# Fewer TensorE tiling changes in a joint image and text attention block: full-size text transposes, adjacent text mods, gate rows beside the text scores, text keys in four row tiles

## The chip, the cores and the metric

The kernel runs on one core of one Trainium2 chip. The time is device microseconds of that core for one execution, as the median of several executions. "Span" is the time of the profiled execution from its first to its last instruction, about 1.8 us shorter than the device time of the same execution.

The records give each TensorE matmul a tile form. In the profile of the kernel before they are 128x128 (687 of 1,051 matmuls), 128x32 (254), 128x64 (76), 64x128 (27), 32x128 (6) and, once, 18x128. In what follows 128x32 is called four column tiles, 64x128 two row tiles and 32x128 four row tiles, because the matmuls of one such form are seen to overlap: four on 128x32 tiles start 2 to 5 ns apart, mostly 3 or 4, and each lasts 286 ns by its modelled end. The change is about how often the form changes.

## The reference, cut to what matters

There are B = 2 batches of Ni = 256 image tokens and Nt = 32 text tokens, D = 1152, all bf16.

```
mod_i = silu(c) @ wmod_img ;  mod_t = silu(c) @ wmod_txt     # shift, scale, gate of each stream
hi = layernorm(x_img) * (1 + sci) + shi ;  ht = layernorm(x_txt) * (1 + sct) + sht
qkvi = hi @ wqkv_img ;  qkvt = ht @ wqkv_txt
scores = concat(qt, qi) @ concat(kt, ki)^T * D**-0.5 ;  p = softmax(scores) ;  a = p @ concat(vt, vi)
out_i = x_img + gai * (ai @ wo_img) ;  out_t = x_txt + gat * (at @ wo_txt)
```

Fourteen matrices of 1152x1152 (2.65 MB each) are read once. That is nearly all of the traffic.

## The kernel before

All weights are loaded by one in-order queue into five slots in on-chip memory, each of which is used several times. A load into a slot is not issued before the last reader of its old content is done; the loads behind it in the queue wait too. In the profile before, the scale rows end at 56.25 us and the load into their slot is issued at 56.29.

```python
    # ... cut: the loads of the image scale and value weights into slots 0 and 1 ...
    w_sh_i = load_w(2, wmod_img, 0)          # first argument: the slot
    w_q_i = load_w(3, wqkv_img, 0)
    w_sh_t = load_rows(0, wmod_txt, 0)
    w_k_i = load_w(4, wqkv_img, D)
    w_sc_t = load_w(1, wmod_txt, D)          # text scale weights
    w_q_t = load_w(2, wqkv_txt, 0)
    w_k_t = load_w(3, wqkv_txt, D)
    w_v_t = load_w(1, wqkv_txt, 2 * D)       # text value weights: the slot of the text scale weights
    w_ga_i = load_w(0, wmod_img, 2 * D)      # image gate weights
    w_ga_t = load_w(2, wmod_txt, 2 * D)
    w_o_i = load_rows(3, wo_img, 0)
    w_o_t = load_rows(1, wo_txt, 0)
```

TensorE's program order is fixed. The text work is hung into the nine blocks of the image query and key projections:

```python
    qk_img(w_q_i, 0, {1: (txt_ln,), ..., 6: (txt_transposes,), 8: (txt_shift_part(6, KT),)})
    qk_img(w_k_i, 1, {1: (txt_shift_split, txt_rows_scale,),
                      6: (txt_rows_shift, txt_cols_shift, txt_modulate),
                      8: (lambda: qk_txt(0, w_q_t),)})
    qk_txt(1, w_k_t)
    # ... cut: helpers ...
    scores_txt()
    scores_img(0)
    img_gate()
    scores_img(1)
    v_txt()
    p_transposes(0)
    txt_gate()
    # ... cut: attn_pair(G[0], G[1]); p_transposes(1); two more pairs; the output projections
```

`txt_rows_scale` multiplies the conditioning vector by the text scale weights: 36 matmuls on 128x32 tiles, 1.3 us. It is the last reader of that slot. `img_gate` does the same with the image gate weights. Transposes are matmuls too: the small ones use 64x128 or 32x128 tiles. In `attn_pair` the text keys are added with two row tiles of 64 rows.

## Time and profile before

| | before |
|---|---|
| time, median (range) | 120.37 us (120.02 to 120.63, 3 runs) |
| span of the profile | 118.6 us |
| TensorE busy | 95% of the span |
| weight stream | about 410 GB/s almost until the last weights |

From the page: the span in 40 slices (TensorE's busy tenths, its granted clock in tenths, the DMA engines' busy tenths, GB/s), then the chain of waits that ended last, by engine.

```profile
PE   4988899999999999999999999999999999999990
PEclk9999999999999999999999999999999999999998
DMA  4999999999999999999999999999999996220223
GB/s 104 382 392 399 404 410 406 413 412 411 411 389 384 413 412 410 405 413 411 412 413 412 410 407 413 412 404 412 405 408 411 412 389 219 109 89 16 99 50 100
...
PE 86%; DMA 8%; DVE 2%; SPq 1%; issue 1%; DVEq 0%
```

After the first slices TensorE never rests, and the chain is almost all TensorE. The stream has no hole either: two resources are full at once, and only one of them is on the chain.

The timeline of the load queue (start and duration of the issue in us, then what is loaded):

```profile
56.29 0.85 SPq L89 DMA_DIRECT2D t<-in_wqkv_txt_dram  x1
62.68 0.82 SPq L89 DMA_DIRECT2D t<-in_wmod_img_dram  x1
```

The text value weights are asked for at 56.29 us, as soon as the scale rows are done; the image gate weights at 62.68. The stream is still busy with the text key weights then.

The timeline of TensorE, some groups (start, us from the first start to the last end, operation, tile form, shape, count):

```profile
46.72 0.43 PE L64 MATMUL tpt<-ident,xn_t 64*128 64x64 bf16 x9
...
54.96 1.29 PE L61 MATMUL gps<-t,sT 128*32 128x288 bf16 x36
...
66.00 0.67 PE L61 MATMUL gps<-hl,pick 128*32 128x288 bf16 x16
...
77.26 3.21 PE L61 MATMUL sps<-qkT 128*32 128x288 bf16 x36
80.40 1.29 PE L61 MATMUL gps<-t,sT 128*32 128x288 bf16 x36
81.62 2.38 PE L61 MATMUL sps<-qkT 128*128 128x288 bf16 x18
...
89.17 0.54 PE L61 MATMUL aps<-pT,v_t 64*128 64x288 bf16 x6
```

In order: the small text transposes, the scale rows (54.96), the shift rows (66.00), the text scores with image scores(0), the image gate rows (80.40), image scores(1), and the text keys of the first pair. None of these lines has an idle time in brackets at its end: TensorE waits for nothing. (Some matmul records can be missing from a trace, so a count may be one or two short.)

The single matmul records of this profile say what a change of form costs here. Successive matmuls start 216 ns apart (512 columns) or 123 ns apart (288 columns). Where the form changes and nothing is waited for, the distance is about 310 ns (309 to 311, from 512 columns) or 219 ns (214 to 219, with 288), so 91 to 96 ns more, and the step after a return to 128x128 is 10 ns longer (226 or 133 ns). That is what was measured; what happens in the engine meanwhile is not shown.

### The profile page before, as it was taken

How to read it: one execution, taken by the hardware profiler on the slowest of the kernel's cores; microseconds unless marked ns; L12 is line 12 of the kernel's file. 1: busy time of each engine (PE TensorE's matmuls, PEld its weight loads, DVE VectorE, ACT ScalarE, POOL GpSimd, SP SyncE). 2: the span in 40 equal slices, each digit the busy share in tenths (PEclk: the TensorE clock that was granted, in tenths of full speed). 3: DMA queues.
4: the chain of work that ended last, by engine and by line, in shares of the span. 5: the costliest groups of instructions: out<-in, count | busy, mean ns of one | idle time of the engine just before them, and what ended most of it. 6: DMA issues, size and time to landing. Idle time of an engine off the chain costs nothing.

```text
span 118.6 us, 2515 instructions
## 1 busy us (share of the span) xinstructions
PE 112.1 (95%) x1051; PEld 64.0 (54%) x1059; DVE 75.3 (63%) x157; ACT 41.8 (35%) x86; POOL 10.3 (9%) x31
## 2 busy tenths in 40 slices
PE   4988899999999999999999999999999999999990
PEld 1335544445674444445444457877876666666660
DVE  2568592063966799999999540048685666666571
ACT  4799620041752524323039233345327620000000
POOL 7110000000000000000000000000409017000000
PEclk9999999999999999999999999999999999999998
DMA  4999999999999999999999999999999996220223
GB/s 104 382 392 399 404 410 406 413 412 411 411 389 384 413 412 410 405 413 411 412 413 412 410 407 413 412 404 412 405 408 411 412 389 219 109 89 16 99 50 100
DMA packets 18613, 40.86 MB, mean 345 GB/s; under 512 B 1019, under 2 KB 1547, under 8 KB 18603
## 3 DMA queue, kind: packets, MB, share of 16 engines
q1 hardware_dynamic: 17728, 39.56, 85.7%
q0 software_dynamic: 480, 0.89, 2.2%
q10 hardware_dynamic: 395, 0.26, 0.7%
q8 instruction: 8, 0.13, 0.4%
q14 instruction: 2, 0.02, 0.0%
HBM read 39.38 MB, written 1.34 MB: 343 GB/s over the span
## 4 chain that ended last, share of the span: by engine, by line
PE 86%; DMA 8%; DVE 2%; SPq 1%; issue 1%; DVEq 0%
PE ps L61 52%; PE vps L61 15%; DMA t<-in_wmod_img_dram 8%; PE gps L61 6%; PE aps L61 6%; PE sps L61 5%; PE sc_ps L61 1%; PE pT_ps L64 1%; SPq L104 1%; DVE tmp L629 1%; DVE o L630 0%; DVE scc L217 0%; SPq L108 0%; PE tpt L64 0%; PE tp L64 0%
## 5 line engine op out<-in xcount | busy, mean ns | idle before, releaser
L61 PE MATMUL ps<-xT_i,t 128*128 128x512 bf16 x157 | 35.6, 380 | 0.3
L61 PEld LDWEIGHTS <-t 128*128 128x128 bf16 x324 | 20.4, 98 | 19.2 <-issue 0.7
L395 DVE SCALAR_TENSOR_TENSOR acc_sh<-t,sTf,acc_sh 128x1152 f32<-128x1152 bf16 x16 | 21.3, 1404 | 0.0
L61 PE MATMUL ps<-t,aT 128*128 128x384 bf16 (+3 forms) x153 | 20.2, 308 | 0.0
L61 PE MATMUL vps<-t,hS_i 128*128 128x512 bf16 (+1 forms) x106 | 17.8, 325 | 0.3 <-DVE hS_i L248 0.2
L61 PEld LDWEIGHTS <-aT 128*128 128x128 bf16 (+1 forms) x153 | 13.0, 101 | 7.1 <-issue 0.5
L61 PEld LDWEIGHTS <-hS_i 128*128 128x128 bf16 x108 | 9.0, 98 | 8.8 <-DVE hS_i L248 0.3
L629 DVE TENSOR_TENSOR tmp<-ps,gb 128x384 bf16<-128x384 f32 (+2 forms) x13 | 6.8, 526 | 6.3 <-PE ps L61 6.3
L346 ACT ACTIVATE qkT<-ps 128x512 bf16<-128x512 f32 (+2 forms) x11 | 6.2, 561 | 12.1 <-PE ps L61 12.1
L61 PE MATMUL wps<-warm 128*128 128x512 bf16 x25 | 7.7, 458 | 1.6 <-DVE unit L132 1.5
L481 POOL DMA_DIRECT2D mod_scratch<-g_sb x4 | 2.5, 634 | 76.6 <-ACT g_sb L174 76.6
L348 ACT CAST qkT<-ps 128x512 bf16<-128x512 f32 (+2 forms) x11 | 5.9, 554 | 8.3 <-PE ps L61 8.3
L172 DVE CAST v_i<-vps 128x512 bf16<-128x512 f32 x5 | 3.5, 692 | 8.2 <-PE vps L61 8.2
L553 DVE TENSOR_TENSOR half<-sps,half 64x288 f32<-64x288 f32 x1 | 0.4, 448 | 9.0 <-ACT half L552 9.0
L587 DVE TENSOR_SCALAR aT<-aps,svc 128x288 bf16<-128x288 f32 x9 | 4.5, 518 | 2.6 <-PE aps L61 2.5
L61 PEld LDWEIGHTS <-sT 128*32 128x32 bf16 x180 | 4.5, 96 | 2.8 <-issue 2.2
L174 ACT CAST v_i<-vps 128x512 bf16<-128x512 f32 x4 | 2.3, 580 | 10.0 <-PE vps L61 10.0
L61 PE MATMUL sps<-qkT 128*128 128x288 bf16 (+1 forms) x54 | 5.6, 288 | 0.0
L61 PEld LDWEIGHTS <-warm 128*128 128x128 bf16 x26 | 2.6, 111 | 5.2 <-issue 2.1
L61 PE MATMUL aps<-pT,v_i 128*128 128x288 bf16 x36 | 5.3, 288 | 0.0
L589 ACT ACTIVATE aT<-aps,svc 128x288 bf16<-128x288 f32 x9 | 4.1, 498 | 3.0 <-PE aps L61 2.9
L61 PE MATMUL gps<-t,sT 128*32 128x288 bf16 x144 | 5.1, 287 | 0.0
(104 smaller groups left out, 108.0 us busy)
## 6 DMA issues: line engine op xcount, KB each, us to landing
t<-in_wqkv_txt_dram SPq DMA_DIRECT2D x3, 2592.0 KB, 16.5
t<-in_wmod_img_dram SPq DMA_DIRECT2D x2, 2592.0 KB, 13.9
t<-in_wqkv_img_dram SPq DMA_DIRECT2D x2, 2592.0 KB, 20.1
t<-in_wmod_txt_dram SPq DMA_DIRECT2D x2, 2592.0 KB, 15.5
t<-in_wmod_txt_dram SPq DMA_DIRECT2D x3, 864.0 KB, 14.7
t<-in_wo_img_dram SPq DMA_DIRECT2D x3, 864.0 KB, 12.3
t<-in_wo_txt_dram SPq DMA_DIRECT2D x3, 864.0 KB, 11.4
t<-in_wqkv_img_dram SPq DMA_DIRECT2D x3, 576.0 KB, 9.2
```

The lines of the kernel that those rows point to most:

```text
L61: return pin(nc.tensor.matmul(*a, **k))
L64: return pin(nc.tensor.transpose(*a, **k))
L104: nc.sync.dma_start(x_i[:, b * TPB:(b + 1) * TPB, :], x_img[b].rearrange("(p t) d -> p t d", t=TPB))
L172: nc.vector.tensor_copy(out_ap, in_ap)
L174: nc.scalar.copy(out_ap, in_ap)
L346: nc.scalar.mul(out_ap, in_ap, SCALE)
L348: nc.scalar.copy(out_ap, in_ap)
L395: pin(eng.scalar_tensor_tensor(acc[:, b, :], w[:, kt, :], sTf[:, kt, b:b + 1], acc[:, b, :], op0=ALU.mult, op1=ALU.add))
L481: nc.gpsimd.dma_start(gsc[si, b, :].rearrange("(g j) -> g j", g=NGG), g_sb[b:P:32, :])
L587: nc.vector.tensor_scalar(dst, tiles[(b, dt)][:], bias, None, op0=ALU.add)
L589: nc.scalar.activation(dst, tiles[(b, dt)][:], ACT.Identity, bias=bias)
L629: nc.vector.tensor_mul(tmp[:, 0:n], ps[:, 0:n], gb[:, b, c0:c0 + n])
```

## The change

The intent is to change the form less often.

- The text is normalised into two halves, one above the other, so that five full transposes replace nine small ones.
- The scale rows go beside the shift rows, both 128x32.
- Image scores(0) come before the text scores, so that text scores and gate rows, both 128x32, are adjacent.
- The probabilities of the text queries are transposed full size, from a zero-padded tile, and both batches one after the other.
- The text keys use four row tiles of 32 rows.

```diff
     def txt_transposes():
-        tpt = ps_tr.tile([P, KT, NTT], bf, tag="tr")
-        for kt in range(KT):
-            tr(tpt[:, kt, :], xn_t[:, kt * P:(kt + 1) * P], ident[0:NTT, 0:NTT])
+        tpt = ps_tr.tile([P, KH, 2, NTT], bf, tag="tr")
+        for k in range(KH):
+            tr(tpt[:, k].rearrange("p h t -> p (h t)"), xn_t[:, k * P:(k + 1) * P], ident[:])
 # ... cut: the two halves of xn_t, the padded tiles and their memsets ...
-    qk_img(w_k_i, 1, {1: (txt_shift_split, txt_rows_scale,),
-                      6: (txt_rows_shift, txt_cols_shift, txt_modulate),
+    qk_img(w_k_i, 1, {1: (txt_shift_split,),
+                      6: (txt_rows_scale, txt_rows_shift, txt_cols_shift, txt_modulate),
 # ... cut: p_transposes with full-size transposes of the text tile ...
-            first = key in t1
-            r0, (b, dt) = 64 * (n % 2), key
-            mm((t1 if first else t0)[key][:], lhsT=v_t[r0:r0 + 64, dt * P:(dt + 1) * P],
-               rhs=pTs[b][r0:r0 + 64, 2, :], start=first, stop=not first, tile_position=(r0, 0))
+            first, (b, dt) = key in t1, key
+            r0 = 64 * (n // 2 % 2) + NT * b
+            mm((t1 if first else t0)[key][:], lhsT=v_t[r0:r0 + NT, dt * P:(dt + 1) * P],
+               rhs=pTs[b][r0:r0 + NT, 2, :], start=first, stop=not first, tile_position=(r0, 0))
-    scores_txt()
     scores_img(0)
+    scores_txt()
     img_gate()
     scores_img(1)
     v_txt()
     p_transposes(0)
+    p_transposes(1)
     txt_gate()
 # ... cut: each attn_pair takes three tiles of each batch ...
```

More of the change, by code (lines that the diff above doesn't have):

```diff
@@ L150 @@
     nc.gpsimd.memset(shT32[:], 0.0)
+    PBW = 3 * P
+    pb_tiles = [act.tile([P, PBW], bf, name="pb%d" % i) for i in range(2 * B)]
+    pb_txt = act.tile([P, PBW], bf, name="pbt")
+    KH = (KT + 1) // 2
+    xn_t = act.tile([P, KH * P], bf)
+    nc.gpsimd.memset(pb_txt[:], 0.0)
+    nc.gpsimd.memset(xn_t[NTT:P, (KT - KH) * P:KH * P], 0.0)
+    for t in pb_tiles:
+        nc.gpsimd.memset(t[:, NI:PBW], 0.0)
+    ident2 = const.tile([P, P], bf)
+    nc.gpsimd.tensor_copy(ident2[:, 0:P - NT], ident[:, NT:P])
+    nc.gpsimd.tensor_copy(ident2[:, P - NT:P], ident[:, 0:NT])
     e18 = small.tile([B * KT, P], f32, bufs=1)
@@ L372, in shift_v_rows @@
         cols["v"] = mod_cols_of(p_sv, "svc")
-    xn_t = act.tile([NTT, D], bf)
     xT_t = act.tile([P, KT, NTT], bf)
@@ L380, in txt_ln @@
         mv = ln_stats(x_t[:, :], NTT)
-        ln_norm(x_t[:, :], mv[0:NTT, 0:1], ln_rstd(mv[0:NTT, 1:2], NTT), NTT, xn_t[:, :])
+        rstd = ln_rstd(mv[0:NTT, 1:2], NTT)
+        for h, (c0, c1) in enumerate(((0, KH * P), (KH * P, D))):
+            ln_norm(x_t[:, c0:c1], mv[0:NTT, 0:1], rstd, NTT, xn_t[NTT * h:NTT * (h + 1), 0:c1 - c0])
     def txt_transposes():
-        tpt = ps_tr.tile([P, KT, NTT], bf, tag="tr")
-        for kt in range(KT):
-            tr(tpt[:, kt, :], xn_t[:, kt * P:(kt + 1) * P], ident[0:NTT, 0:NTT])
-        nc.scalar.copy(xT_t[:], tpt[:])
+        tpt = ps_tr.tile([P, KH, 2, NTT], bf, tag="tr")
+        for k in range(KH):
+            tr(tpt[:, k].rearrange("p h t -> p (h t)"), xn_t[:, k * P:(k + 1) * P], ident[:])
+        for h, (k0, k1) in enumerate(((0, KH), (KH, KT))):
+            nc.scalar.copy(xT_t[:, k0:k1, :], tpt[:, 0:k1 - k0, h, :])
     def vec_part(eng, w, acc, r0, r1, bs):
@@ L514 @@
     pbs = {}
-    PBW = 3 * P
-    pb_tiles = [act.tile([P, PBW], bf, name="pb%d" % i) for i in range(2 * B + 1)]
-    for t in pb_tiles:
-        nc.gpsimd.memset(t[:, NI:PBW], 0.0)
     def softmax_tile(sps, qn, key, parts):
@@ L527, in softmax_tile @@
         nc.vector.reciprocal(rs[0:qn, :], rs[0:qn, :])
-        pb = pb_tiles[len(pbs)]
+        pb = pb_txt if key == "t" else pb_tiles[key[0] * TPB + key[1]]
         nc.vector.tensor_scalar_mul(pb[0:qn, 0:NI], e[0:qn, 0:NI], rs[0:qn, :])
@@ L558, in p_transposes, with one @@
     def p_transposes(b):
-        pT_ps = ps_tr.tile([P, 3, NTOK], bf, tag="tr")
-        for qi in range(TPB):
-            qp = qpos[b][qi]
-            pb = pbs[(b, qi)]
-            for kj in range(3):
-                tr(pT_ps[:, kj, qp:qp + P], pb[:, kj * P:(kj + 1) * P], ident[:])
-        qp = qpos[b][2]
-        pb = pbs["t"]
-        r0 = NT * b
-        for kj in range(3):
-            tr(pT_ps[:, kj, qp:qp + NT], pb[r0:r0 + NT, kj * P:(kj + 1) * P], ident[r0:r0 + NT, r0:r0 + NT])
+        pT_ps = ps_tr.tile([P, 8 * P], bf, tag="tr")
+        def one(kj, pb, qp, perm):
+            o = kj * NTOK + qp
+            tr(pT_ps[:, o:o + P], pb[:, kj * P:(kj + 1) * P], perm[:])
+        for kj in range(3):
+            if b:
+                one(kj, pbs["t"], qpos[b][2], ident2)
+            for qi in range(TPB):
+                one(kj, pbs[(b, qi)], qpos[b][qi], ident)
+            if not b:
+                one(kj, pbs["t"], qpos[b][2], ident)
+        pT_v = pT_ps[:, 0:3 * NTOK].rearrange("p (k n) -> p k n", k=3)
         pT = work.tile([P, 3, NTOK], bf, tag="pT")
         if b == 0:
-            nc.vector.tensor_copy(pT[:], pT_ps[:])
+            nc.vector.tensor_copy(pT[:], pT_v)
         else:
-            nc.scalar.copy(pT[:], pT_ps[:])
+            nc.scalar.copy(pT[:], pT_v)
         pTs[b] = pT
@@ L603, in attn_pair @@
         attn_evac(t1)
+    scores_img(0)
     scores_txt()
-    scores_img(0)
     img_gate()
@@ L610 @@
     p_transposes(0)
+    p_transposes(1)
     txt_gate()
-    G = [[(b, dt) for dt in range(d0, d0 + 3)] for b in range(B) for d0 in range(0, KT, 3)]
-    attn_pair(G[0], G[1])
-    p_transposes(1)
-    attn_pair(G[2], G[3])
-    attn_pair(G[4], G[5])
+    for d0 in range(0, KT, 3):
+        attn_pair(*[[(b, dt) for dt in range(d0, d0 + 3)] for b in range(B)])
     def out_img(i, chunks, parts=None):
```

## The prediction

> **What bounds the kernel now.** TensorE: busy 95% of the 118.6 us span (page, part 1), 86% of the chain of waits; from 14.8 to 115 us that chain is almost TensorE alone. The weight stream is nearly as tight: about 410 GB/s in almost every slice up to 95 us (page, part 2), one in-order queue of 2.65 MB matrices, about 6.5 us each.
>
> **What a tiling change costs here.** In the single matmul records the usual start-to-start time is 216 ns (512 columns) or 123 ns (288). Where the tile form changes (128x128 to 128x32, 128x64, 64x128 or back) it is 310 or 219, and after returning to 128x128 the next step is 10 ns longer. So 93 to 106 ns per change. [...]
>
> **Savings on TensorE, all on the chain:**
> - Text transposes: 9 of 30 ns and two changes become 5 full ones of 56 ns: 0.18 us.
> - Text scale rows beside shift rows: one pair of changes less: 0.20 us.
> - Image scores(0), text scores, gate rows: two changes fewer, and a 90 ns wait of text scores for the last key copy goes: 0.29 us.
> - Probability transposes: 1.22 us become 18 x 56 ns and one change: 0.11 us.
> - Text keys in 4 row tiles: 3 packs of 119 ns become 2, three times: 0.36 us; a 74 ns wait for the second transposed tile also goes.
>
> Sum about 1.2 us. VectorE and ScalarE gain small pieces (a split normalisation, a split copy) off the chain; GpSimd's new memsets (estimate 1.9 us, from 0.2 us per 128x128 memset) fit its 2.6 us idle before the silu copies.
>
> **What it moves badly.** Text scale rows move from 55.0 us to the sixth key block. They are the last reader of the weight slot that the text value weights reload. Before, that load was issued at 56.3 us, well before the stream finished the text key weights (64.6). After, scale rows run at 64.5 to 65.8 us, so the load is issued at 65.8; an idle queue needs 0.85 us from issue to first packet (output stores). The stream stands still 2.1 to 2.3 us, and everything behind it is later by that. The image gate weights landed at about 79.3 us (last packet 77.7 plus the 1.6 us that other loads take to signal), 1.1 us before TensorE used them (80.4). After, they land at about 81.5, while TensorE, having saved 0.67 us, arrives at 79.7: a new stall of about 1.7 us on the chain. Text gate weights (85.7 to 87.9) are asked for at about 88.8: no second stall. Output weights have over 3 us of slack.
>
> **Sum.** -1.2 + 1.7 to 1.9 = +0.6 us: 120.9 us. Range 119.3 to 121.8. Faster by over 2%: 0.02; within 2%: 0.95; slower by over 2%: 0.03.
>
> **What would show it.** Load of the text value weights issued near 65.8 us; a dip in the GB/s row at 65 to 67 us; gate-row matmuls waiting for the DMA of image gate weights about 1.7 us; text-key groups 0.14 us from first to last start rather than 0.26; no 151 ns step before small transposes.
>
> **What would make it wrong.** If the stream does not stall (load released earlier, or TensorE slowed first by another wait), the result is near 119.2. If four row tiles do not run together, 0.4 us less gain. If the second transposes wait for their probabilities, or the text shift rows for the halves that VectorE finishes at 65.5 us, some tenths more.

The sum has all its terms: -1.2 us of savings and +1.7 to 1.9 us of waiting give +0.6 us.

## The result, and the profile after

The changed kernel takes 123.44 us (123.14 to 123.69, 4 runs) beside 120.41 us before (120.02 to 120.63, 4 runs). The ratio is 1.0254, with a 95% interval of 1.0216 to 1.0292: slower by 2.5%. A ratio here is the mean time of one kernel's runs over the mean of the other's runs of the same rounds, so it is not quite the ratio of the medians. All runs count, but their mean granted clock is 0.981 to 0.986.

The same parts of the page, after:

```profile
PE   5978999999999999999999999928999999999990
PEclk9999999999999999999999999996799999999998
DMA  4999999999999999999992999999999997311213
GB/s 129 375 401 394 405 409 409 412 412 412 411 370 412 412 412 408 409 412 412 412 406 83 289 409 404 406 410 412 405 410 410 410 382 291 121 44 58 97 48 97
...
PE 73%; DMA 21%; DVE 2%; SPq 1%; issue 0%; DVEq 0%
```

Four things are new. The stream falls to 83 and 289 GB/s in the slices at 64 to 70 us. TensorE has a hole near 80 us ("28" in its row). Directly after the hole the granted clock drops ("67"). The chain now has 21% of DMA rather than 8%.

The load queue after:

```profile
65.93 0.37 SPq L89 DMA_DIRECT2D t<-in_wqkv_txt_dram  x1
66.47 1.67 SPq L89 DMA_DIRECT2D t<-in_wmod_img_dram  x1
```

The text value weights are asked for 9.6 us later than before.

TensorE after, the same groups:

```profile
46.74 0.44 PE L64 MATMUL tpt<-ident,xn_t 128*128 128x128 bf16 x5
...
64.60 1.29 PE L61 MATMUL gps<-t,sT 128*32 128x288 bf16 x36
65.71 0.66 PE L61 MATMUL gps<-hl,pick 128*32 128x288 bf16 x16
...
76.87 3.09 PE L61 MATMUL sps<-qkT 128*128 128x288 bf16 x36
82.64 1.88 PE L61 MATMUL gps<-t,sT 128*32 128x288 bf16 x36 [2.68 <-DMA t<-in_wmod_img_dram]
84.45 3.41 PE L61 MATMUL sps<-qkT 128*128 128x288 bf16 x18
...
93.53 0.42 PE L61 MATMUL aps<-pT,v_t 32*128 32x288 bf16 x6
```

The scale rows end at about 65.9 us and free the slot there. The gate rows start at 82.64 us after 2.68 us of idle time, which the DMA of the image gate weights ended. (Idle time is counted from the modelled end of the last matmul. Counted from the moment when the next matmul could have started, 79.80 us by the last start at 79.67 us and the usual 123 ns, the wait is 2.84 us, as in the sum below.) The gate rows then take 1.88 us rather than 1.29, and image scores(1) 3.41 us rather than 2.38.

The time around the hole, in stretches of 3.41 us whose ends are those of the halved stretch in the clock records. The columns are the stretch; the busy us and instruction counts of TensorE, its weight loads, VectorE, ScalarE and GpSimd; the granted clock; the DMA share; GB/s:

```profile
79.76:83.18 3.42, 0.74 (x26) 0.48 (x24) 2.33 (x10) 1.61 (x5) 0.00 (x0) 1.00 1.04 411
83.18:86.59 3.41, 3.41 (x37) 1.91 (x27) 0.54 (x3) 0.40 (x1) 1.33 (x2) 0.50 1.05 416
86.59:90.00 3.41, 3.41 (x46) 2.84 (x46) 2.16 (x9) 1.19 (x4) 0.05 (x1) 1.00 1.03 401
```

The clock is exactly half for one stretch of 3.41 us and whole before and after. In it, image scores(1) start 240 ns apart rather than 123.

**The sum, from the single matmul records of the two profiles.** The savings came as costed, or somewhat larger.

| piece | predicted | measured |
|---|---|---|
| text transposes (677 to 495 ns between image matmuls) | -0.18 us | -0.18 us |
| scale rows beside shift rows (2.23 to 2.02 us) | -0.20 | -0.21 |
| end of key projections to readiness for the gate rows (3.26 to 2.96 us) | -0.29 | -0.31 |
| probability transposes (1.22 to 1.11 us) | -0.11 | -0.11 |
| attention pairs without transposes (6.34 to 5.79 us) | -0.43 | -0.55 |
| wait at the gate rows (ready at 79.80, start at 82.64) | +1.7 | +2.84 |
| gate rows to text values (3.53 to 5.15 us), at half clock | none | +1.62 |
| sum | about +0.6 | +3.1 |

The measured sum of +3.1 us agrees with the difference of the medians, 3.0 us, and of the two spans, 3.2 us.

### The profile page after: what moved, and what is told of

It is laid out like the page before. It is cut to its first block, busy times and chain, and to the rows that moved or that the text cites. A ratio compares the mean times of both kernels' runs of the same rounds, so it can differ in the third digit from the quotient of the medians.

```text
span 121.8 us, 2520 instructions
## 1 busy us (share of the span) xinstructions
PE 113.0 (93%) x1055; PEld 64.5 (53%) x1055; DVE 75.5 (62%) x158; ACT 42.0 (34%) x87; POOL 11.2 (9%) x34
## 4 chain that ended last, share of the span: by engine, by line
PE 73%; DMA 21%; DVE 2%; SPq 1%; issue 0%; DVEq 0%
PE ps L61 42%; DMA t<-in_wmod_img_dram 21%; PE vps L61 15%; PE gps L61 6%; PE aps L61 5%; PE sps L61 3%; PE sc_ps L61 1%; PE pT_ps L64 1%; SPq L104 1%; DVE tmp L640 1%; DVE o L641 0%; DVE scc L229 0%; SPq L108 0%; PE tp L64 0%; PE wps L61 0%
## 5 line engine op out<-in xcount | busy, mean ns | idle before, releaser
L532 DVE TENSOR_REDUCE nmx<-sps 128x1 f32<-128x288 f32 x4 | 1.8, 448 | 11.9 <-PE sps L61 11.9
L61 PE MATMUL gps<-t,sT 128*32 128x288 bf16 x144 | 5.7, 308 | 2.7 <-DMA t<-in_wmod_img_dram 2.7
L61 PE MATMUL sps<-qkT 128*128 128x288 bf16 (+1 forms) x54 | 6.5, 313 | 0.0
L61 PEld LDWEIGHTS <-qkT 128*128 128x128 bf16 (+1 forms) x54 | 4.3, 106 | 2.1 <-issue 0.7
```

The costliest lines, as they stand in the source:

```text
L61: return pin(nc.tensor.matmul(*a, **k))
L532: nc.vector.reduce_max(nmx[0:qn, :], sps[0:qn, :], axis=AX.X, negate=True)
```

## The experiments

The theory (T) has four links. The moved scale rows free a weight slot late. The stream therefore runs dry. The image gate weights land late and TensorE waits for them. The wait halves TensorE's clock. The rivals put the time elsewhere: R1, the new order brings the gate rows too early by itself; R2, the row tiles or full transposes are slow; R3, the slow matmuls after the gate rows have another cause than the wait.

All experiments computed correct results.

### 1. The changed kernel with the scale rows put back

```diff
-    qk_img(w_k_i, 1, {1: (txt_shift_split,),
-                      6: (txt_rows_scale, txt_rows_shift, txt_cols_shift, txt_modulate),
+    qk_img(w_k_i, 1, {1: (txt_shift_split, txt_rows_scale,),
+                      6: (txt_rows_shift, txt_cols_shift, txt_modulate),
```

> The changed kernel with one part undone: the text scale rows go back to the second key block. Theory T (late release of a weight slot stalls the weight stream, image gate weights land late, TensorE waits about 2.7 us and its clock is halved for 3.4 us afterwards): the load of the text value weights is issued near 56.2 us, no dip in the weight stream at 64 to 68 us, image gate weights land near 79.3 us, no wait at the gate rows, clock 1.0 throughout; time 119.0 to 119.6 us. Rival R1 (the new order of scores and gate rows brings the gate rows to the weights too early by itself): a wait of over 1 us stays at the gate rows and the time stays above 121.5 us. Rival R2 (four row tiles or the full transposes cost the time): the time stays above 122 us with no wait at the gate rows.

It took 119.67 us (119.39 to 119.92, 6 runs), ratio 0.9937 (0.9914 to 0.9961). The load was issued at 55.95 us, the stream kept its pace and the mean clock was 0.999 or 1.0 in all runs. R2 falls, and R1 as the main cause. A trace of R1 is there: the gate weights landed at 80.00 us in this profile and the gate rows still started about 0.24 us later than they could have. The time is 0.1 us over the expected range. The changed kernel reaches the gate rows so early that the gate weights have no slack left.

### 2. The kernel before with the scale rows moved, and nothing else

The diff is that of experiment 1 in reverse, on the kernel before.

> The kernel before with this one part of the change alone: the text scale rows moved beside the shift rows. Theory T: the load of the text value weights is issued near 66 us, the stream falls below 100 GB/s at about 65 to 67 us, image gate weights land near 82.7 us, TensorE waits 2.2 to 2.5 us at the gate rows, the clock is halved for 3.4 us; time 123.6 to 124.4 us, slower than the whole change. Rivals R1 and R2 (the cause is in scores, gate order, transposes or row tiles): 120.2 us, the 0.2 us of the two tiling changes saved.

The profiled run took 122.69 us, mean clock 1.0. It has the late issue (65.87 us) and this wait:

```profile
82.67 1.29 PE L61 MATMUL gps<-t,sT 128*32 128x288 bf16 x36 [2.56 <-DMA t<-in_wmod_img_dram]
```

This one part makes the kernel before over 2 us slower (by this single run, so the size is rough), and it alone brings the stall. R1 and R2, which expected 120.2 us, fail. The halved clock that was expected is not in the profiled run. The three other runs took 124.58 to 125.44 us at a mean clock of 0.986; they lie over 1.5% above the fastest run, so they count as slow and no comparison is rested on them. Why this run escaped is taken up after experiment 6.

### 3. The changed kernel with the gate weights loaded first

```diff
-    w_v_t = load_w(1, wqkv_txt, 2 * D)
     w_ga_i = load_w(0, wmod_img, 2 * D)
+    w_v_t = load_w(1, wqkv_txt, 2 * D)
```

> The changed kernel, everything kept, but the load of the image gate weights is put before that of the text value weights in the queue; its slot is free at about 62.6 us, before the stream runs dry. Theory T: no gap of the stream or one under 0.5 us, image gate weights land near 73 us, text value weights near 79.5 us, needed at about 83 us; no wait at the gate rows, clock 1.0; time 118.8 to 119.4 us, the best of all. Rivals R1 and R2: no change by this beyond the wait; under R2 above 121 us.

It took **118.81 us** (118.64 to 119.48, 6 runs), ratio 0.9879 (0.9851 to 0.9906). That is 1.2% faster than the kernel before and the best of all; the interval is clear of 1. Its load queue, and TensorE at the gate:

```profile
62.75 0.37 SPq L89 DMA_DIRECT2D t<-in_wmod_img_dram  x1
65.43 0.37 SPq L89 DMA_DIRECT2D t<-in_wqkv_txt_dram  x1
...
76.37 3.09 PE L61 MATMUL sps<-qkT 128*128 128x288 bf16 x36
79.17 1.39 PE L61 MATMUL gps<-t,sT 128*32 128x288 bf16 x36
```

The scale rows are as late as in the changed kernel (64.10 us, in a profile that runs 0.5 us ahead of the changed kernel's), and the load that needs their slot is as late (65.43 us). But another load, whose slot is free at 62.75 us, is now ahead of it and keeps the queue fed. The gate weights land at 72.90 us, the text value weights at 79.61 us, and nothing waits for either. Here the late slot was harmless because it was not the next in line.

### 4. Idle matmuls in the wait

```diff
     scores_img(0)
     scores_txt()
+    idle_ps = ps_mm.tile([P, 512], f32, tag="mm")
+    for _ in range(11):
+        mm(idle_ps[:], lhsT=warm[:, 0:P], rhs=warm[:], start=True, stop=True)
     img_gate()
```

> The changed kernel with 11 idle matmuls of 512 columns (2.4 us, result unused) on TensorE between the text scores and the gate rows, where it waits for the weights. Theory T (the lost clock follows from the idle wait): the gate rows still start near 82.6 us, idle before them under 0.5 us, clock 1.0 afterwards, image scores(1) back to 123 ns per matmul from 240; time about 121.8 us, 1.6 us faster than the changed kernel. Rival R3 (the slow matmuls after the gate have another cause than the wait, such as the traffic or the new order): image scores(1) stay near 240 ns and the time stays near 123.4 us.

It took 122.15 us (121.81 to 122.70, 4 runs), ratio 1.0158, and the clock was 0.999 or 1.0 in all runs:

```profile
79.76 2.55 PE L61 MATMUL idle_ps<-warm 128*128 128x512 bf16 x10
82.57 1.29 PE L61 MATMUL gps<-t,sT 128*32 128x288 bf16 x36 [0.26 <-DMA t<-in_wmod_img_dram]
83.79 2.38 PE L61 MATMUL sps<-qkT 128*128 128x288 bf16 x18
```

The gate rows start as late as in the changed kernel (82.57 against 82.64 us), yet they and image scores(1) are back at 1.29 and 2.38 us. (Eleven idle matmuls ran; the record of one is missing.) Doing useless work made the kernel about 1.2 us faster than the changed one (ratio 1.0158 against 1.0254 to the same kernel). R3 falls: without the idle time the slow matmuls are gone.

### 5. The scale rows one key block earlier

```diff
-                      6: (txt_rows_scale, txt_rows_shift, txt_cols_shift, txt_modulate),
+                      5: (txt_rows_scale,),
+                      6: (txt_rows_shift, txt_cols_shift, txt_modulate),
```

> The changed kernel with the text scale rows one key block earlier (the fifth rather than the sixth, 1.95 us earlier). Theory T, as a matter of dose: the load of the text value weights is issued near 64.0 us, the stream loses about 1.4 us rather than 3.3, image gate weights land near 80.7 us, TensorE comes to the gate rows near 80.0 and waits 0.5 to 0.8 us, too short to halve the clock; time 119.8 to 120.4 us. A theory in which any move of the rows away from the second block, or the merged rows themselves, cost the time, expects over 122 us or under 119.6.

It took 120.56 us (120.08 to 121.28, 4 runs), ratio 1.0013 (0.9975 to 1.0052), clock 1.0 in all runs.

```profile
63.87 0.37 SPq L89 DMA_DIRECT2D t<-in_wqkv_txt_dram  x1
...
81.91 1.29 PE L61 MATMUL gps<-t,sT 128*32 128x288 bf16 x36 [1.85 <-DMA t<-in_wmod_img_dram]
```

The direction is right, the size is a miss. The issue came 2.06 us earlier than in the changed kernel, but the gate weights landed only 0.73 us earlier (81.86 against 82.59 us), and TensorE waited 1.85 us rather than 0.5 to 0.8. Even this wait did not halve the clock. Packet counts show what the stream lost. At the full rate of these profiles (about 412 GB/s) the queue moved about 45 packets of 2,304 bytes per quarter microsecond. In the changed kernel the count begins to fall at about 63.75 us, before the text key weights have landed: of the queue's 16 engines the first signalled its share at 64.01 us and the last at 66.58 us. The first packets of the next load came 1.0 us after its issue, but the rate was near full only 2.5 us after it, at 68.5 us. Two stretches of the changed kernel (columns as above; the kernel before has 412 and 409 GB/s in them):

```profile
63.50:66.00 2.50, 2.50 (x54) 1.55 (x56) 2.20 (x2) 2.27 (x4) 0.00 (x0) 1.00 0.39 155
66.00:68.50 2.50, 2.50 (x26) 1.08 (x16) 1.97 (x5) 0.04 (x1) 0.00 (x0) 1.00 0.56 117
```

In the first 1.6 us of the new load a packet took 176 ns on average, rather than 93 at full rate; why is not shown. In experiment 5 the issue at 63.87 us fell just as the first engines ran dry, and the rate was near full from about 66.75 us. The packets missing from the full rate between 63 and 72 us give the loss in each profile. The lead is how long before the first engine's signal for the text key weights the next load was issued. Seven profiles stand here; the other six give the same picture:

| profile | lead | stream lost |
|---|---|---|
| before | 7.84 us | 0.0 us |
| experiment 3 | 1.55 | 0.3 |
| two row tiles (experiment 8) | 1.15 | 0.7 |
| scale rows back (experiment 8) | 0.85 | 0.8 |
| experiment 5 | 0.45 | 1.7 |
| three idle matmuls (experiment 6) | -1.21 | 2.8 |
| the changed kernel | -1.92 | 3.4 |

From these rows, a lead of about 2 us would cost nothing; this is an estimate, since no profile lies between 1.55 and 7.84 us. The stream of experiment 5 lost half of what the changed kernel's lost, yet the gate weights landed only 0.73 us earlier. Fifteen of their sixteen engines had signalled by 81.02 us and the last at 81.86 us; why that one was late is not shown.

The 16 engines finish the text key weights 2.6 us apart in the changed kernel, and 2.2 us apart in the kernel before (64.14 to 66.37 us), where the stream does not stall. So the uneven finish is not itself a loss: the stream lost 0.0 us where the next load had been issued 7.84 us before the first engine's signal, and 3.4 us where it was issued 1.92 us after it.

### 6. Fewer idle matmuls: how long a wait halves the clock

As experiment 4, with `range(3)`, then with `range(6)`.

> As e4_warm_wait with 3 idle matmuls (0.65 us) in place of 11: TensorE's idle time before the gate rows is about 2.0 us in place of 2.7, and nothing else differs from the changed kernel. If the halved clock depends on the length of the idle time, as e5_rows_fifth_block (2.0 us idle, clock 1.0 in 4 of 4 runs) suggests: clock 1.0 and 121.8 to 122.4 us, as e4. If any long wait halves it, or the order of scores and gate rows does: mean clock near 0.984 and 123.4 us.

> As e9_short_warm_wait with 6 idle matmuls in place of 3: TensorE idle about 1.4 us before the gate rows. The clock records of the profiles so far are whole multiples of 3.41 us; where the clock halved, the 3.41 us just before held 2.7 us (the changed kernel) and 2.1 us (e9) of idle time, and where it did not at most 1.8 us (e5) or 1.6 us (e2's profiled run, whose idle time fell across a boundary). If it is the idle share of one such stretch that counts, with a limit between 1.8 and 2.1 us, 1.4 us can never reach it: clock 1.0 in all 6 runs, 121.8 to 122.4 us. If any wait in this place can halve it: mean clock near 0.985 in some of the runs and 123.4 us.

With three idle matmuls: 123.47 us (123.00 to 123.65, 4 runs), mean clock 0.982 to 0.986 in all runs. The expectation failed: 2.08 us of idle time, hardly more than the 1.85 us of experiment 5, did halve the clock. With six: 122.02 us (121.71 to 122.43, 6 runs), clock 0.996 to 1.0, as expected.

The clock records of the profiles explain the difference. Between the first rise of the clock and the last fall, all lengths are whole multiples of 3.41 us: 33 of them in the kernel before; 23, then 1 at half clock, then 10 in the changed kernel; 11 and 22 to 34 in the other profiles. So in these profiles the clock changed only on a grid of 3.41 us, and its phase differs from profile to profile: the halved stretch begins at 83.18 us in the changed kernel and at 82.50 us with three idle matmuls. These are the stretches of the grid that hold most of the wait, and the next ones: with three idle matmuls, then in experiment 5, then the three stretches around the wait of experiment 2 (columns as in the stretches above).

```profile
79.09:82.50 3.41, 1.28 (x24) 0.47 (x17) 2.32 (x10) 1.61 (x5) 0.00 (x0) 1.00 1.04 411
82.50:85.91 3.41, 3.41 (x43) 2.00 (x36) 0.73 (x3) 0.40 (x1) 0.64 (x1) 0.50 1.06 416
```

```profile
80.15:83.56 3.41, 1.65 (x40) 1.23 (x41) 2.32 (x10) 1.72 (x6) 0.00 (x0) 1.00 1.04 411
83.56:86.98 3.42, 3.42 (x42) 2.75 (x42) 1.77 (x8) 1.27 (x5) 1.38 (x2) 1.00 1.04 407
```

```profile
77.62:81.03 3.41, 2.49 (x24) 1.68 (x18) 2.32 (x9) 1.61 (x5) 0.00 (x0) 1.00 1.04 409
81.03:84.45 3.42, 1.78 (x41) 1.34 (x42) 1.46 (x7) 0.99 (x3) 0.00 (x0) 1.00 1.04 412
84.45:87.86 3.41, 3.41 (x43) 2.76 (x43) 1.61 (x7) 1.18 (x4) 1.38 (x2) 1.00 1.04 406
```

A stretch with 2.08 us or more of idle time was followed by one at half clock, and a stretch with 1.76 us or less by one at full clock:

| profile | most idle time in one stretch of 3.41 us | clock in the next |
|---|---|---|
| the changed kernel | 2.68 us | 0.5 |
| three idle matmuls | 2.08 us (2.13 in the view, where the record of one idle matmul is missing) | 0.5 |
| experiment 5 | 1.76 us | 1.0 |
| experiment 2 | 1.64 us (its 2.56 us lay across a boundary: 0.92 + 1.64) | 1.0 |
| six idle matmuls | 1.33 us | 1.0 |

By these waits the limit in this kernel lies between 1.76 and 2.08 us of 3.41. The ends of the profiles, where TensorE has finished, are further points. In the kernel before, the stretch with the last matmul holds 2.00 us of idle time, and the clock halves after it:

```profile
114.03:117.44 3.41, 1.41 (x18) 1.15 (x15) 2.02 (x6) 0.00 (x0) 0.00 (x0) 1.00 0.27 87
117.44:118.61 1.17, 0.00 (x0) 0.00 (x0) 0.00 (x0) 0.00 (x0) 0.00 (x0) 0.50 0.00 0
```

So does it after 2.08 us at the end of the changed kernel, but not after 1.72 us at the end of the run with three idle matmuls. The limit measured here is then between 1.76 and 2.00 us, from these profiles alone. It also says why experiment 2's profiled run escaped: its wait was as long as that of the changed kernel, but it fell across two stretches. For runs without a trace only the mean clock is known, so that their phase did it is an inference. One thing does not fit well: if the phase fell evenly, a wait of 2.08 us would be cut by a boundary and escape in about half of the runs (an estimate from these limits), but with three idle matmuls all four runs were halved. Chance, or phases that are not even, or a finer rule: that stays open.

### 7. The load order on the kernel before

The swap of experiment 3 applied to the kernel before.

> The kernel before with the load of the image gate weights put before that of the text value weights, as in e3_gate_load_first, and nothing of the change. Theory T: TensorE never waited for either, so the time stays within 0.3 us of 120.4 and e3's gain is that of the change itself. Rival R4 (e3 is fast because of its load order, whatever the change does): about 119 us.

It took 120.44 us (119.99 to 120.93, 6 runs), ratio 1.0003 (0.9977 to 1.0029). The load order by itself gives nothing. The 1.2% of experiment 3 is the change's own gain, which its own stall had hidden.

### 8. Parts of the gain, taken out of experiment 3 one at a time

Text keys back in two row tiles (`r0 = 64 * (n % 2)`, 64 rows):

> e3_gate_load_first with the text keys back in 2 row tiles of 64 rows. If four row tiles run together as costed: three packs instead of two in each of three pairs, text-key groups 0.26 us from first to last start rather than 0.14; 0.36 us slower than e3, 119.1 to 119.3 us. If they do not: no difference.

Text scores back before image scores(0):

> e3_gate_load_first with the old order: text scores, image scores(0), gate rows. As costed: two more tiling changes of 0.1 us and a wait of 0.09 us of the text scores for the last key copy, the gate rows start 0.29 us later against the end of the key projections; about 119.1 us.

Scale rows back in the second key block:

> e1_rows_back with the image gate weights loaded before the text value weights, which is e3_gate_load_first without the merged text rows. In e1 the gate rows still waited about 0.24 us for their weights; here they do not wait. Against e3 it has two tiling changes more: 0.2 us slower than e3, 118.9 to 119.3 us, and 0.2 to 0.5 us faster than e1.

| kernel | time, median | ratio to before (95%) | from the last key projection to the first output projection |
|---|---|---|---|
| before | 120.36 us | 1 | 18.13 us |
| experiment 3 | 118.81 | 0.9879 (0.9851 to 0.9906) | 17.15 |
| two row tiles | 119.66 | 0.9924 (0.9904 to 0.9945) | 17.53 |
| text scores first | 119.10 | 0.9898 (0.9874 to 0.9923) | 17.48 |
| scale rows back | 119.47 | 0.9915 (0.9895 to 0.9935) | 17.15 (the scale rows lie outside) |

The text-key group with two row tiles, against 0.42 us with four in the profile after:

```profile
89.23 0.54 PE L61 MATMUL aps<-pT,v_t 64*128 64x288 bf16 x6
```

Inside the stage the row tiles are worth 0.37 us and the order 0.33 us, as costed (0.36 and 0.29). Of the expected times, that of the text scores was met, and those of the other two were missed: 119.66 us against 119.1 to 119.3, and 119.47 against 118.9 to 119.3. The times of whole runs point the same way but cannot measure such sizes: they put the two row tiles at 0.5 us and the merged rows at 0.4 us rather than 0.2, with intervals of about 0.3 us, and these kernels ran in different submissions from experiment 3. For the merged rows the records of one profile are the better measure (0.21 us).

## Why the prediction was wrong

The mechanism was foreseen and every link of it was found: the slot, the late issue (predicted 65.8 us, measured 65.93), the hole in the stream, the wait for the image gate weights. The savings were right to about 0.2 us. The second full transposes and the shift rows did not wait, and the text gate rows had no second stall. Still the time, 123.44 us, lies well outside the range of 119.3 to 121.8, and "slower by over 2%" had been given 0.03. Two terms were wrong.

- **"The stream stands still 2.1 to 2.3 us": it lost 3.3 to 3.4 us.** The gate weights landed at 82.59 us, against 79.25 before and about 81.5 predicted. The end of the old load was right: its last packets, though spread out to 66.2 us, add up to a full-rate stream that ends at 64.5 us (predicted 64.6). The restart was wrong. The prediction let the new load run at full rate from its first packet, at about 66.7 us. In fact the first packet came 1.0 us after the issue (the 0.85 us had been read from output stores: 0.83 to 0.86 us for the three of 288 KB in the profile before), and the rate climbed to full only at 68.5 us; counted in packets, the new load ran as if at full rate from 67.9 us. Those stores show no such climb: in the two quarter microseconds from 1.0 us after the issue they moved 37 to 44 packets each, near the full rate of 45. The wait became 2.84 us in place of 1.7.
- **The clock was left out.** The prediction counted a wait as costing its own length. It cost 1.62 us more, because over half of a 3.41 us stretch was idle (2.68 us) and the next ran at half clock. The profile before showed this only at its very end (the "8" that closes its clock row), since TensorE did not rest before. By the limit measured in experiment 6 (1.76 us of idle time in a stretch did not halve the clock, 2.00 us did), a wait of 1.7 us would not have halved it, and one of 2.84 us could.

With both terms at their measured size, -1.36 + 2.84 + 1.62 = +3.1 us is the result. The two errors are not independent: the first lengthened the wait beyond the limit of experiment 6 and so made the second possible.

The swap in experiment 3 needs one moved line. The change was a gain of 1.2% with a resource conflict attached, not a bad idea.

## What to carry to other kernels

Before you move an operation later, ask what it is the last reader of, and which load, and which loads behind it, wait for that buffer; then feed the queue with whatever is free, and issue each load early: here about 2 us (an estimate from the table in experiment 5) before the first engine of the load ahead is done. Where a long TensorE wait can't be avoided, fill most of it with throw-away matmuls: here a wait of 2.84 us cost another 1.62 us in halved clock afterwards, with 1.33 us of it left idle (six idle matmuls) the clock stayed whole, and with 2.08 us (three) it halved. The savings of about 0.1 us per tiling change were real here and added up, but read them from the single records of one profile and not from the times of whole runs.
